# Where the sums of tokens, a product, copies of x and the counts of C stand in a Fourier-mixing and MLP kernel

## The chip, the cores and the metric

The kernel runs on 1 core of one Trainium2 chip. The metric is the device time of one execution in microseconds (us); the table below has the median of three runs. The program is compiled ahead; every engine (TensorE or PE, VectorE or DVE, ScalarE or ACT, GpSimd or POOL, SyncE or SP) works through its own queue of instructions in a fixed order and waits on semaphores.

## The reference

All in float32, with x of 2048 tokens by 576. `A_*` are the matrices of a discrete Fourier transform over the hidden and over the sequence dimension, `B_w1` is 576 by 4608, `B_w2` 4608 by 576.

```python
xn = _layernorm(x)                                   # no scale, no bias
a = einsum("bsd,ed->bse", xn, dft_hid_re)
b = einsum("bsd,ed->bse", xn, dft_hid_im)
y = einsum("ts,bse->bte", dft_seq_re, a) - einsum("ts,bse->bte", dft_seq_im, b)
h = maximum(einsum("bsd,df->bsf", xn, w1), 0)
return x + y + einsum("bsf,fd->bsd", h, w2)
```

## The kernel before, in words

Every float32 operand is split into two float16 parts, hi and lo, and each product is three float16 matmuls (hi by hi, hi by lo, lo by hi), summed in PSUM.

The tokens are 16 tiles of 128, in 4 groups of 4 tiles (`G` = 512 tokens). The hidden width of the MLP is cut into 9 blocks of 512. The outer loop, `steps`, runs over blocks b = 0 to 8 and inside over groups g = 0 to 3. At step (b, g) the program issues the first products `mlp1` of (b, g), interleaved with the second products `mlp2` of the step before it.

- `mlp2(b, g, n)`, n = 0 to 6, are the seven products of a Strassen-Winograd scheme. Products 0, 2, 3 and 6 are evacuated from PSUM by ScalarE (line 603), 1, 4 and 5 are added by VectorE (line 606). Products that share a PSUM place must wait until the one before them on that place has been read: 2 waits for the evacuation of 0, 4 for that of 2, and 6 for VectorE's addition of 4. GpSimd then adds the results to a buffer in DRAM, `spill` (line 609), which starts as a copy of x (`copy_x`, line 802, on SyncE's queue).
- `mlp1_out` (lines 388 to 404) turns the PSUM of `mlp1` into h and its four sums: ScalarE writes hi, VectorE lo.
- In blocks 0 and 1 `mlp1` is plain. From block 2 (`BB`) on it too is a Strassen-Winograd product (`pair_products`, line 515), and for that it needs sums of quarters of the transposed tokens. `sums_x(g)` makes them for group g: four sums, each 2 or 3 VectorE operations (lines 472 to 476), one ScalarE operation for hi (line 455) and one VectorE operation for lo (line 460). They go to `acc`, whose old content has been spilled by then. For groups 0 to 2 the temporary lies in a part of `dbuf`, and all of it is issued in block 1, one piece for each piece of work that takes a token from `owed_t`. For group 3 the temporary is `tsum`, the single buffer (tag `first`) that the counts use, and its pieces are issued in block 2 (`t_sum`).
- The counts: before the sequence transform the program needs a scale for each of 16 units of the matrices C. `first_c(m)` loads a block of C into the single buffer, `sum_c(m)` sums its absolute values on ScalarE (line 1012). `passes` is the list of such pairs. It starts in block 1, pauses while group 3's sums use the buffer (`PAUSE`), and goes on with two passes a group from step (2, 2).
- `prepare_block(b + 1)` is a list of small pieces that load, scale and split the weights of the next block: `load_w1`, `max_w1` (line 115), an all-reduce on GpSimd (line 121), `split_w1` (line 184), `load_w2`, `sum_w2` (line 683) and so on. `work()` issues the next piece.
- Step (0, 2), n = 2 in the loop, also normalizes tiles 12 to 15 (`normalize`, lines 258 and 259; `remainder`, lines 265 and 268) and transposes them by DMA (line 282).

The order in each queue is made by a scheduler from the order in which the program issues work. `tc.issue_after(x)` and `behind(key)` only keep what is inside from standing ahead of x, or of the last instruction recorded under that key; they add no wait of their own.

Of the kernel before, what the change touches and what calls it, by code (L numbers as in the profile page):

```python
# [49 lines left out]
def kernel(  # L50
# [47 lines left out]
    def load_raw(key, src, shape):  # L98
        r = raws[key] = raw.tile(shape, F32, tag="raw", name="raw_" + "_".join(map(str, key)))
        nc.sync.dma_start(r, src)  # L100
# [337 lines left out]
    def sums_x(g):  # L438

        if g < NG - 1:

            f = [w[:, 2 * KT * P :][:, : 2 * GH] for w in w1bufs[2:]]
        else:
            w = mlp.tile([P, HK, P], F32, tag="first", name="tsum", bufs=1)
            w = w.rearrange("p a b -> p (a b)")
            f = [w[:, k : k + 2 * GH] for k in (0, 2 * GH)]
        f = [w.rearrange("p (k t) -> p k t", t=GH) for w in f]  # L450
        tt = nc.vector.tensor_tensor

        def high(q):
            with tc.issue_after(gates[g][0]):
                nc.scalar.activation(xsums[g][:, q, 0], f[q % 2], AF.Copy)

        def low(q):
            hi, lo = (xsums[g][:, q, n] for n in range(2))
            with tc.issue_after(gates[g][1] if g < NG - 1 else order["vfree"]):
                tt(lo, f[q % 2], hi, ALU.subtract)  # L460

        for q, (head, tail) in enumerate((
            ((0, 1), (0, 0)), ((1, 1), None), ((1, 0), None), ((1, 1), (0, 1)),
        )):
            if q > 1:
                low(q - 2)
            t = f[q % 2]
            h, l = halves(g, head)
            with behind("vfree" if g == NG - 1 else None):
                if tail:  # L470
                    h2, l2 = halves(g, tail)
                    tt(t, h, h2, ALU.subtract)
                    tt(t, t, l2, ALU.subtract)
                else:
                    tt(t, h, f[1 - q % 2], ALU.subtract)
                tt(t, t, l, ALU.add)
# [136 lines left out]
    def max_w1(b, f):  # L613

        i, r = divmod(f, 2)
        if f == 0:
            mx["w1", b], sc["w1", b], pw["w1", b] = cell("mw1"), cell("sw1"), cell("pw1")
        if r == 0:
            mx["f", b] = cell("mf", 2)
        with behind("vfree" if b >= BB else "vfree" if f > 1 and b else ("sh", 12) if b  # L620
                    else ("sh", 1) if f > 1 else None):
            magnitude(mx["f", b][:, r : r + 1], raws["w1", b, i][:, r * KT : (r + 1) * KT])
        if r:
            if b:
# [3 lines left out]
            nc.vector.tensor_reduce(m, mx["f", b], AX.X, ALU.max)  # L628
# [282 lines left out]
    copy_x(2)  # L911
    mlp2(0, 0, 0)
# [13 lines left out]

    owed_t = [1] * 10 * (NG - 1)
# [73 lines left out]
    def first_c(m):  # L1001
        n, q = divmod(m, 4)
        f = firsts[m] = mlp.tile([P, HK, P], F32, tag="first", name=f"f{n}_{q}", bufs=1)
        with tc.issue_after(order["td"]):
            nc.sync.dma_start(f, blocks_c(n)[q])

    def sum_c(m):
# [19 lines left out]
    for n in range(2, len(steps)):  # L1027
# [26 lines left out]
        if b >= BB:  # L1054
# [10 lines left out]
            for do, q in (  # L1065
                (first, P1), (first, P2), (m, 0), (end, 0), (first, P6),
                (brief, 1), (first, P5), (end, 0), (later1, P2), (m, 1), (t_sum, 0),
                (ready, 1), (second, P1), (first, P7), (ready, 1), (m, 2), (second, P2),
                (t_sum, 0), (count, 0), (brief, 1), (first, P3), (first, P4), (later1, P7), (m, 3),
                (second, P6), (later1, P3), (later1, P4), (later2, P2), (brief, 1), (m, 4),  # L1070
                (t_sum, 0), (second, P5), (ready, 1), (m, 5), (end, 0), (second, P7),
                (t_sum, 0), (end, 0), (brief, 1), (m, 6), (count, 0), (brief, 2),
# [5 lines left out]
        for i in range(NF):  # L1078
            if n == 2:
                ps.append(early.pop(0) if early else mlp1(b, g, i))  # L1080
# [17 lines left out]
            if n == 2:  # L1098
                if i == 2:
                    todo += prepare_block(1)  # L1100
                for _ in range(6):
                    work()
                continue
            if b:
                work()
            for q in range(2 * i, min(2 * i + 2, 7)):
                mlp2(pb, pg, q)
                if b:
                    if owed_t:
                        owed_t.pop()  # L1110
                        next(tq, None)
# [3 lines left out]
            if b and i == 3 and owed_t:  # L1115
                owed_t.pop()
# [249 lines left out]
```

## Time and profile before

| what | value |
|---|---|
| median of 3 runs (1254.05 to 1255.16) | 1254.05 us |
| the profiled execution's own time | 1253.33 us |
| its span | 1251.6 us |
| TensorE busy | 1229.5 us (98%) |
| VectorE busy | 1008.3 us (81%) |
| ScalarE busy | 704.4 us (56%) |
| GpSimd busy | 158.1 us (13%) |
| granted TensorE clock, mean | 1.0 |

Times in the profile count from the start of the span. A row of the timeline has a start, a length, the engine, the line of the program, the operation, output and inputs, sizes, a count, and in brackets how long the engine had been idle before it and which instruction ended that. "x28" merges 28 instructions that follow one another. A row's length reaches past the start of the next one, since instructions overlap a little.

### The profile page before, as it was taken

The page shows a single profiled execution, that of the slowest core. Times are in us where ns is not written, and L with a number is a line of the kernel's source. Part 1 is how long each engine was busy: PE and PEld are TensorE (multiplying, and loading weights), DVE is VectorE, ACT ScalarE, POOL GpSimd, SP SyncE. Part 2 cuts the span into 40 slices and gives each one's busy share as a digit, 9 for nine tenths or more (in the row PEclk, how much of TensorE's full clock was granted, in tenths as well). Part 3 has the DMA queues.
Part 4 walks back from the last instruction along what each step waited for, and adds up shares of the span by engine and source line. Part 5 has one row for each costly group of instructions (what it writes and reads, how often), then busy time and mean ns, then how long its engine had stood idle before and what let it go on. Part 6 is the DMA issues. An engine that isn't in the chain of part 4 may idle for free.

```text
span 1251.6 us, 25268 instructions
## 1 busy us (share of the span) xinstructions
PE 1229.5 (98%) x10269; PEld 980.5 (78%) x10269; DVE 1008.3 (81%) x1919; ACT 704.4 (56%) x1192; POOL 158.1 (13%) x207
## 2 busy tenths in 40 slices
PE   8999999899999999999999999999999999999998
PEld 7655557788888888888888888877777777777776
DVE  8998986988878788788787878557787878888885
ACT  5655565566667666766766766546543333333332
POOL 2421121212121111111121212200000000000000
PEclk9999999999999999999999999999999999999999
DMA  8895475456667665766576666630053434443420
GB/s 311 166 183 113 94 136 122 78 110 143 132 120 170 126 150 116 137 140 137 117 160 136 140 147 117 114 89 1 1 173 120 136 109 155 128 132 123 137 87 20
DMA packets 80324, 157.28 MB, mean 126 GB/s; under 512 B 22224, under 2 KB 41168, under 8 KB 80208
## 3 DMA queue, kind: packets, MB, share of 16 engines
q1 hardware_dynamic: 57424, 113.20, 28.2%
q0 software_dynamic: 22784, 42.48, 25.1%
q8 instruction: 80, 1.31, 0.4%
q14 instruction: 36, 0.29, 0.1%
HBM read 104.53 MB, written 51.90 MB: 125 GB/s over the span
## 4 chain that ended last, share of the span: by engine, by line
PE 81%; DVE 13%; DMA 2%; ACT 2%; issue 2%; SPq 0%; POOL 0%; DVEq 0%; ACTq 0%; POOLq 0%
PE p L1298 26%; PE p L592 23%; PE bank L515 22%; PE pd L1169 8%; DMA raw_w<-in_w_dram 1%; PE p L344 1%; DVE w2s L184 1%; DVE c_mf L115 1%; DVE h L393 1%; DVE st L207 1%; DVE w1buf L184 1%; DVE h L404 1%; DVE h L537 0%; DMA f<-in_cre_dram 0%; DVE dbuf L258 0%
## 5 line engine op out<-in xcount | busy, mean ns | idle before, releaser
L592 PE MATMUL p<-w2s,h 128*128 128x288 f16 x3024 | 409.3, 286 | 9.8 <-ACT acc L603 2.3
L592 PEld LDWEIGHTS <-h 128*128 128x128 f16 x3024 | 295.4, 98 | 87.4 <-issue 12.7
L1298 PE MATMUL p<-R,cs 128*128 128x288 f16 x2688 | 329.4, 286 | 0.0
L1298 PEld LDWEIGHTS <-cs 128*128 128x128 f16 x2688 | 263.0, 98 | 66.3
L183 ACT ACTIVATE cs<-c,sc_c 128x1024 f16<-128x1024 f32 x112 | 125.2, 1144 | 196.7 <-DVE c L1231 72.6
L184 DVE SCALAR_TENSOR_TENSOR cs<-c,sc_c,cs 128x1024 f16<-128x1024 f32 x112 | 141.0, 1282 | 54.4 <-ACT cs L183 54.4
L515 PEld LDWEIGHTS <-w1buf 128*128 128x128 f16 x1600 | 156.5, 98 | 23.9 <-issue 2.8
L515 PEld LDWEIGHTS <-dbuf 128*128 128x128 f16 x1200 | 117.4, 98 | 15.8
L515 PE MATMUL bank<-xT,w1buf 128*128 128x256 f16 x832 | 109.8, 273 | 0.0
L515 PE MATMUL bank<-acc,w1buf 128*128 128x256 f16 x768 | 102.3, 273 | 2.1 <-DVE acc L545 1.1
L1169 PE MATMUL pd<-dbuf,xT 128*128 128x288 f16 x832 | 103.8, 286 | 0.0
L537 DVE TENSOR_TENSOR h<-s,h 128x1024 f16<-128x1024 f32 x56 | 68.6, 1224 | 37.9 <-ACT h L534 37.9
L1169 PEld LDWEIGHTS <-xT 128*128 128x128 f16 x832 | 80.8, 98 | 22.0 <-issue 1.9
L609 POOL DMA_DIRECT2D spill<-dbuf x70 | 61.1, 879 | 244.7 <-DVE dbuf L606 218.8
L522 ACT ACTIVATE h<-acc 128x256 f16<-128x256 f32 x112 | 46.0, 411 | 65.9 <-DVE acc L545 64.4
L515 PE MATMUL bank<-xT,dbuf 128*128 128x256 f16 x624 | 82.3, 273 | 0.0
L534 ACT ACTIVATE h<-s 128x1024 f16<-128x1024 f32 x56 | 59.2, 1056 | 36.8 <-DVE s L529 36.5
L515 PE MATMUL bank<-acc,dbuf 128*128 128x256 f16 x576 | 76.6, 273 | 0.0
L1304 DVE SCALAR_TENSOR_TENSOR o<-p,us_c,o 128x288 f32<-128x288 f32 x112 | 57.6, 514 | 12.9 <-PE p L1298 12.5
L1012 ACT ACTIVATE f<-f 128x1024 f32<-128x1024 f32 x60 | 62.8, 1046 | 2.5 <-DMA f<-in_cre_dram 2.5
L603 ACT ACTIVATE dbuf<-p,c_ub 128x576 f32<-128x576 f32 x70 | 51.2, 734 | 22.4 <-PE p L592 21.2
L609 POOL DMA_DIRECT2D spill<-sum x42 | 36.8, 877 | 183.5 <-DVE sum L606 164.9
(169 smaller groups left out, 1531.8 us busy)
## 6 DMA issues: line engine op xcount, KB each, us to landing
spill<-dbuf POOLq DMA_DIRECT2D x70, 288.0 KB, 5.2
c<-in_cre_dram SPq DMA_DIRECT2D x32, 512.0 KB, 4.3
c<-in_cim_dram SPq DMA_DIRECT2D x32, 512.0 KB, 4.8
f<-in_cre_dram SPq DMA_DIRECT2D x30, 512.0 KB, 5.4
f<-in_cim_dram SPq DMA_DIRECT2D x30, 512.0 KB, 5.6
spill<-sum POOLq DMA_DIRECT2D x42, 288.0 KB, 4.5
raw_w<-in_w_dram SPq DMA_DIRECT2D x17, 640.0 KB, 5.8
raw_w<-in_w_dram SPq DMA_DIRECT2D x18, 576.0 KB, 4.4
```

Of the source, the lines that this page charges most:

```text
L183: nc.scalar.activation(hi, src, AF.Copy, scale=s).ins,
L184: nc.vector.scalar_tensor_tensor(lo, src, s, hi, ALU.mult, ALU.subtract).ins,
L515: nc.tensor.matmul(ps, l, r, start=first and m == 0, stop=m == len(todo) - 1, skip_group_check=not first,)
L534: order["s"] = nc.scalar.activation(hi_s, st[:, 1:], AF.Copy).ins
L537: order["lo"] = nc.vector.tensor_tensor(lo_s, st[:, 1:], hi_s, ALU.subtract).ins
L592: order["pe"] = nc.tensor.matmul(ps[:, c], h[:, x, qa, c * P : (c + 1) * P], w[:, y, qb], start=first and i == 0 and j == 0, stop=i == NQ ...
L603: freed(nc.scalar.activation(o, ps, AF.Copy, scale=us[b]))
L609: nc.gpsimd.dma_start(spill[g, row, col], o, accum_op=ALU.add)
L1012: nc.scalar.activation(f, f, AF.Abs, scale=2.0**-10, accum_out=sums_c[:, n, q : q + 1])
L1169: nc.tensor.matmul(ps[j], xT[g][:, kx, c * P : (c + 1) * P], dsp[j][:, hl, k], start=(t % 2 == 0 and n == 0), stop=(t % 2 == 1 and n == le ...
L1298: nc.tensor.matmul(ps, w[:, a, k], r[:, c, rq], start=first and k == 0 and j == 0, stop=k == HK - 1 and j == 2, skip_group_check=not first,)
L1304: order["o"] = nc.vector.scalar_tensor_tensor(o, ps, us["c"][:, n : n + 1], o, ALU.mult, ALU.add).ins
```

## The change: five edits to the order of work

1. At step (0, 2) products 0 and 1 of `mlp2(0, 1)` are issued ahead of the last `mlp1(0, 2, 3)`. Tile 15's normalization stands behind the evacuation of that product 0 (`after="free"`), and the pieces of `work()` are 1 at i = 2 and 11 at i = 3 in place of 6 at each. The first `max_w1` of block 1 stands behind tile 15's remainder (`("E", 15)`) in place of the statistics (`("sh", 12)`).
2. `copy_x(3)` is issued next to `copy_x(2)`, ahead of the loads of w1 of block 1.
3. The sums of all four groups use the temporary in `dbuf`, and are all issued in block 1: one after each of the seven `mlp2` of a step, and 1 and 2 more at i = 1 and i = 3, so ten a step. `t_sum` and `owed_t` are gone.
4. The first count's load stands behind the loads of w2 of block 1 (`order["loads"]`) in place of the last transpose.
5. The counts have no pause. They begin at step (1, 2), i = 3, run two a group from step (2, 0) on, and one more pass stands in the tail behind product 3.

```diff
@@ load_raw
-        nc.sync.dma_start(r, src)
+        ins = nc.sync.dma_start(r, src).ins
+        if key[:2] == ("w2", 1):
+            order["loads"] = ins
@@ sums_x
-        if g < NG - 1:
-
-            f = [w[:, 2 * KT * P :][:, : 2 * GH] for w in w1bufs[2:]]
-        else:
-            w = mlp.tile([P, HK, P], F32, tag="first", name="tsum", bufs=1)
-            w = w.rearrange("p a b -> p (a b)")
-            f = [w[:, k : k + 2 * GH] for k in (0, 2 * GH)]
-        f = [w.rearrange("p (k t) -> p k t", t=GH) for w in f]
+        f = [
+            w[:, 2 * KT * P :][:, : 2 * GH].rearrange("p (k t) -> p k t", t=GH) for w in w1bufs[2:]
+        ]
...
-            with tc.issue_after(gates[g][1] if g < NG - 1 else order["vfree"]):
+            with tc.issue_after(gates[g][1]):
                 tt(lo, f[q % 2], hi, ALU.subtract)
...
-            with behind("vfree" if g == NG - 1 else None):
@@ max_w1
-        with behind("vfree" if b >= BB else "vfree" if f > 1 and b else ("sh", 12) if b
+        with behind("vfree" if b >= BB else "vfree" if f > 1 and b else ("E", 15) if b
                     else ("sh", 1) if f > 1 else None):
@@ ahead of the loop
     copy_x(2)
+    copy_x(3)
     mlp2(0, 0, 0)
...
-    owed_t = [1] * 10 * (NG - 1)
@@ first_c
-        with tc.issue_after(order["td"]):
+        with behind("loads"):
             nc.sync.dma_start(f, blocks_c(n)[q])
@@ passes
-    PAUSE = 4 + 2 * NG
     passes = [
-        lambda m=m: (sum_c(m - 1) if m not in (4, PAUSE) else None, first_c(m))
-        for m in range(4, 4 * len(units))
+        lambda m=m: (sum_c(m - 1) if m > 4 else None, first_c(m)) for m in range(4, 4 * len(units))
     ]
-    passes.insert(2 * NG, lambda: sum_c(PAUSE - 1))
@@ the loop, blocks from BB on
-            t_sum = lambda q: b == BB and g < NG - 1 and next(tq, None)
-            count = lambda q: (b, g) >= (BB, NG - 2) and passes and passes.pop(0)()
-            if (b, g) == (BB, 0):
-                passes.pop(0)()
+            count = lambda q: passes and passes.pop(0)()
...
@@ the loop, blocks 0 and 1
             if n == 2:
+                if i == 3:
+                    mlp2(pb, pg, 0)
+                    mlp2(pb, pg, 1)
                 ps.append(early.pop(0) if early else mlp1(b, g, i))
...
-                normalize(t)
+                normalize(t, after="free" if i == 3 else None)
...
-            if n == 2 and i == 3:
-                mlp2(pb, pg, 0)
-                mlp2(pb, pg, 1)
...
-                if i == 2:
-                    todo += prepare_block(1)
-                for _ in range(6):
-                    work()
+                if i > 1:
+                    todo += prepare_block(1) if i == 2 else []
+                    for _ in range(1 if i == 2 else 11):
+                        work()
...
-                    if owed_t:
-                        owed_t.pop()
-                        next(tq, None)
+                    next(tq, None)
...
-            if b and i == 3 and owed_t:
-                owed_t.pop()
+            for _ in range((0, 1, 0, 2)[i] if b else 0):
                 next(tq, None)
...
-            if n > 3 and i % 2 and passes:
+            if (n, i) > (6, 1) and i % 2 and passes:
                 passes.pop(0)()
         if n == 2:
-            copy_x(3)
             for q in range(2, 7):
...
@@ the tail
         if ends:
             ends.pop(0)()
+        if q == 3 and passes:
+            passes.pop(0)()
```

More of the change, by code (lines that the diff above doesn't have):

```diff
@@ L468, in sums_x @@
             h, l = halves(g, head)
-            with behind("vfree" if g == NG - 1 else None):
[L470 to L476, printed above, removed]
+            if tail:
+                h2, l2 = halves(g, tail)
+                tt(t, h, h2, ALU.subtract)
+                tt(t, t, l2, ALU.subtract)
+            else:
+                tt(t, h, f[1 - q % 2], ALU.subtract)
+            tt(t, t, l, ALU.add)
             yield
@@ L1060 @@
             brief = lambda q: [work(True) for _ in range(q)]
[L1061 to L1064 removed]
+            count = lambda q: passes and passes.pop(0)()
             for do, q in (
                 (first, P1), (first, P2), (m, 0), (end, 0), (first, P6),
[L1067 removed]
+                (brief, 1), (first, P5), (end, 0), (later1, P2), (m, 1),
                 (ready, 1), (second, P1), (first, P7), (ready, 1), (m, 2), (second, P2),
[L1069 removed]
+                (count, 0), (brief, 1), (first, P3), (first, P4), (later1, P7), (m, 3),
                 (second, P6), (later1, P3), (later1, P4), (later2, P2), (brief, 1), (m, 4),
[L1071 to L1072 removed]
+                (second, P5), (ready, 1), (m, 5), (end, 0), (second, P7),
+                (end, 0), (brief, 1), (m, 6), (count, 0), (brief, 2),
                 (second, P3), (second, P4), (later2, P7), (later2, P3), (later2, P4), (brief, 1),
```

## The prediction

> **What bounds the kernel now.** I read the page's busy shares first, then a table of busy time by stage, then TensorE's rows in order of time for every gap, and last VectorE's and ScalarE's rows around each gap.
>
> ```profile
> PE 1229.5 (98%) x10269; PEld 980.5 (78%) x10269; DVE 1008.3 (81%) x1919; ACT 704.4 (56%) x1192; POOL 158.1 (13%) x207
> ```
>
> TensorE (PE) is busy for 98% of the span, and the change gives it exactly the same matmuls; only 14 of them move. What can change is the time in which it waits. The table by stage (columns: stretch, its length, then busy us of PE, weight loads, DVE, ACT and POOL, the granted clock, the DMA share, GB/s) shows where that is:
>
> ```profile
> 84.00:106.00 22.00, 21.40 (x134) 12.48 (x133) 18.85 (x43) 12.11 (x21) 4.24 (x6) 1.00 0.70 183
> 106.00:154.00 48.00, 45.95 (x282) 26.59 (x281) 46.61 (x87) 26.12 (x44) 9.04 (x9) 1.00 0.58 112
> 154.00:177.00 23.00, 22.23 (x140) 13.34 (x140) 18.71 (x39) 14.97 (x26) 4.18 (x6) 1.00 0.61 123
> 177.00:205.00 28.00, 27.99 (x190) 18.03 (x188) 22.22 (x45) 17.26 (x28) 6.25 (x8) 1.00 0.67 127
> 205.00:250.00 45.00, 41.32 (x352) 34.39 (x352) 36.88 (x81) 24.94 (x52) 7.66 (x10) 1.00 0.49 92
> 250.00:805.00 555.00, 554.33 (x4805) 469.59 (x4804) 448.40 (x988) 376.30 (x734) 97.60 (x125) 1.00 0.65 135
> ```
>
> PE idles 0.60, 2.05, 0.77 and 0.01 us in the four stretches up to 205, 3.68 us from 205 to 250, and 0.67 us in the 555 us behind them. VectorE (DVE) has only 3.15, 1.39 and 4.29 us free in the first three, 8.83 us in all: block 1 is nearly bound by VectorE. The granted clock is 1.00 in every stretch, so no part of the argument hangs on it. The gaps that the edits touch, in PE's order of time (columns: start, length, engine, line, operation, count, and in brackets the idle time before it with its releaser):
>
> ```profile
> 64.94 6.21 PE L344 MATMUL p<-xT,w1buf 128*128 128x512 f16 x28
> 70.98 3.10 PE L592 MATMUL p<-w2s,h 128*128 128x288 f16 x24
> 75.63 1.63 PE L592 MATMUL p<-w2s,h 128*128 128x288 f16 x12 [1.54 <-ACT acc L603]
> ...
> 154.01 1.63 PE L592 MATMUL p<-w2s,h 128*128 128x288 f16 x12 [1.07 <-DVE dbuf L606]
> ...
> 172.81 1.63 PE L592 MATMUL p<-w2s,h 128*128 128x288 f16 x12 [0.76 <-ACT sum L603]
> ...
> 220.93 1.63 PE L592 MATMUL p<-w2s,h 128*128 128x288 f16 x12 [1.62 <-DVE sum L606]
> ...
> 223.98 0.81 PE L515 MATMUL bank<-acc,w1buf 128*128 128x256 f16 x6 [0.54 <-DVE half L124]
> ...
> 246.89 0.81 PE L515 MATMUL bank<-acc,w1buf 128*128 128x256 f16 x6 [1.14 <-DVE acc L545]
> ```
>
> **Edit 1: group 1's first products ahead of the third group's last.** The 28 matmuls at 64.94 are `mlp1(0,2,2)` and `mlp1(0,2,3)`; the 24 behind them are products 0 and 1 of `mlp2(0,1)`. The second half of the 28, some 3.0 us, moves behind the 24. Products 0 and 1 then end at about 71.0 instead of 74.0, their evacuations have 3.0 us more before product 2, and the 1.54 us at 75.63 goes; in ScalarE's queue the first evacuation now stands ahead of the normalizations. What is late next is product 6, which adds to the bank that VectorE's L606 of product 4 must first read. VectorE's rows there:
>
> ```profile
> 82.18 0.82 DVE L606 SCALAR_TENSOR_TENSOR acc<-p,c_ub,acc 128x576 f32<-128x576 f32 x1
> 82.91 1.23 DVE L404 TENSOR_TENSOR h<-s,h 128x1024 f16<-128x1024 f32 x1
> ```
>
> In the built order of the changed kernel the 1024-wide L404 that starts at 82.91 stands ahead of this L606, and two tiny scale operations stand behind it. Back to back the next operation starts some 0.1 us before such a row ends, so L404 takes 1.13 us of the queue, less about 0.14 for the two: L606 starts 1.0 us later, at 83.2, if VectorE has no gap before it in either kernel (its rows just ahead show none). Product 6, for which PE without its earlier waits is ready near 80, starts when that L606 ends: at about 84.1 instead of 83.1 (82.18 + 0.82, and a little). **So this edit, alone, moves a wait to VectorE and costs 1.0 us at that point.** The gates of `max_w1` (behind E of tile 15) and of `normalize(15)` (behind the evacuation) only set this order; tile 15's transposes come no later by my count, so they add nothing. If VectorE's own waits on ScalarE's normalizations show up, the cost grows to at most the 1.54 us that went.
>
> **Edit 2: the copies of x ahead of w1's loads.** On SyncE's queue the four `copy_x(3)` and the first count load stand ahead of w2's loads; the changed queue has the copies at the end of the transposes of group 2, ahead of w1's loads, and the count load behind w2's. The rows of SyncE's queue, of ScalarE's second sum over w2, and of what VectorE then waits for:
>
> ```profile
> 79.93 3.76 SPq L802 DMA_DIRECT2D spill<-in_x_dram  x4
> 83.74 0.60 SPq L1005 DMA_DIRECT2D f<-in_cre_dram  x1
> 85.75 5.62 SPq L100 DMA_DIRECT2D raw_w<-in_w_dram  x2
> ...
> 97.44 1.16 ACT L683 ACTIVATE j<-raw_w 128x1152 f32<-128x1152 f32 x1 [2.04 <-DMA raw_w<-in_w_dram]
> ...
> 99.22 0.69 DVE L393 SCALAR_TENSOR_TENSOR h<-p,h 128x512 f16<-128x512 f32 x1 [1.88 <-ACT h L392]
> ...
> 120.29 0.82 DVE L115 TENSOR_REDUCE c_mf<-raw_w 128x1 f32<-128x640 f32 x1 [0.97 <-DMA raw_w<-in_w_dram]
> ```
>
> The second w2 load is issued near 91 (85.75 + 5.62) and lands just before 97.44, some 6.2 us, with copies and a count load queued ahead of it. The page's row of such loads has a median of 4.4 us to landing:
>
> ```profile
> raw_w<-in_w_dram SPq DMA_DIRECT2D x18, 576.0 KB, 4.4
> ```
>
> At between 4.4 and 5.5 us it lands 1 to 2 us earlier, and ScalarE's queue behind it is free sooner. The 1.88 us gap then closes, because VectorE, 1.0 us behind and with more sums ahead, gets there at about 98.2, after ScalarE. Of the 3.15 us of VectorE's idle time from 84 to 106 I leave 0.4. The 1.39 us from 106 to 154 stays (0.97 of it waits for w1's load, which is tied to a buffer that VectorE frees). The copies themselves now run ahead of w1's loads, which wait there for buffers that VectorE has yet to free; nothing else waits for them. Cost there 0; what it would be if they held w1's loads up is bounded by their own 3.76 us of issue, and VectorE's first use of w1 lies far behind.
>
> **Edit 3: all sums of tokens in block 1.** The fourth group's sums are 14 more VectorE operations 512 wide and 4 on ScalarE, moved from block 2 into block 1; the counts that ran in block 1 leave ScalarE.
>
> ```profile
> L476 DVE TENSOR_TENSOR dbuf<-dbuf,xT 128x512 f32<-128x512 f32 x12 | 8.2, 687 | 0.1
> ...
> 130.33 1.29 DVE L460 TENSOR_TENSOR acc<-dbuf,acc 128x512 f16<-128x512 f32 x2
> ```
>
> One takes 0.69 us, and in a pair the second adds 0.60, so I count 0.60 in a dense queue: 8.4 us. What matters is how much more stands ahead of each L606 on which PE waits. By the built order it is: 2.7 us more ahead of the L606 behind the gap at 154.01 (four sums and a 256-wide operation), and 7.5 us more ahead of the one that releases the next product 6, which starts near 177 (172.81, 12 matmuls and 13 more; thirteen sums, less one such operation). Against that stands idle time that goes: by 154, 3.15 falling to 0.4 (edit 2), so 2.75 us; the two cancel, and the gap at 154.01 stays as it is. By 177, 2.75 plus the 4.29 of 154 to 177, which are waits on ScalarE that VectorE, being later, no longer meets (three of ScalarE's counts are gone from there): 7.0 us against 7.5, so 0.5 us late; the 0.76 us at 172.81, an evacuation that in the changed order stands ahead of ScalarE's L402, goes. I take **0 for everything up to 177**, with bounds of -2.0 (every gap up to there but one closes) and +7.5 (no idle time goes). From 177 to 205 VectorE has 5.8 us free, which covers the last 0.9 us of sums.
>
> **Block 2 without the sums.** Here the sums shared the count's single buffer.
>
> ```profile
> 210.86 1.06 ACT L1012 ACTIVATE f<-f 128x1024 f32<-128x1024 f32 x1 [2.46 <-DMA f<-in_cre_dram]
> ...
> 212.04 0.69 DVE L472 TENSOR_TENSOR tsum<-xT 128x512 f32<-128x512 f16 x1 [2.95 <-ACT f L1012]
> ```
>
> VectorE stood 2.95 us behind a count, which stood 2.46 us behind its load; VectorE is late from there on, and PE waits on it at 220.93, 223.98 and 246.89: 1.62 + 0.54 + 1.14 = 3.3 us. With the buffer left to the counts, VectorE waits for none of them, and it has 8.4 us less to do. The pattern becomes that of 250 to 805 (two counts a group), where PE idles 0.67 us in 555. I take **-3.3**, between 0 and -3.6.
>
> **Counts later.** One more pass runs at the very end: the last count's load now follows the count before it, some 9 us later than now, and the count ends near 816.
>
> ```profile
> 818.55 0.50 ACT L1189 ACTIVATE c<-pd,c_rho 128x288 f32<-128x288 f32 x1 [4.95 <-DMA spill<-sums]
> ```
>
> ScalarE's next work waits until 818.55 for the last spill anyway, so the cost is 0; if that cover is gone it is at most the 1 us or so by which the count's load slows that spill, and PE needs those banks only with the next pair of tiles.
>
> **The sum.** Profiled execution 1253.33 us (span 1251.6 and 1.7 around it), 0.7 below the median of the runs, 1254.05. 0 - 3.3 + 0 = -3.3, laid on the median: **1250.7 us**.
>
> **Rivals.**
>
> *VectorE bounds block 1, and the end is later.* The waits of VectorE from 84 to 177 do not shrink, because they hang on ScalarE and on loads. Each microsecond of the 8.8 that stays beyond 1.3 (8.8 less 7.5) goes onto PE by 177. If all stay: +7.5 - 3.3 = +4.2, 1258.3 us. It is slower by over 2.5 us once some 7 of the 8.8 remain. For it: VectorE's 97% from 106 to 154. Against: the largest wait follows the w2 load, which the edit frees, and ScalarE sheds its counts. Chance 0.16.
>
> *Block 2 keeps its waits.* Counts now run there two to a group, and a count that waits for its load holds ScalarE's evacuations. Then 0 in place of -3.3: 1254.0 us. Against: the stretch from 250. With half of it, or half the first rival, the time stays within 2.5 us of before; chance 0.22.
>
> *More goes than I count.* Product 6 waits no longer than now, and the gaps at 154 and 172 close: -2.0 - 3.3 and the 1.0 of edit 1: 1247.8 us. Chance 0.10.
>
> *GpSimd is held up by the added sums.*
>
> ```profile
> L121 POOL PARTITION_ALL_REDUCE top<-c_mw x24 | 9.8, 408 | 83.6 <-DVE c_mw L628 44.8 <-ACT j L683 38.9
> ```
>
> VectorE waits for such a reduction of 0.41 us before it scales each weight; five of these fall among the sums. Should each be held for one 0.69 us sum, VectorE is 3.4 us later by 177 and the gain is gone: 1254.1 us. [...] Chance 0.04.
>
> *The change doesn't do what it says.* The order is set by a scheduler; but the built order has all sums of tokens ahead of block 2's first product. Chance 0.01.
>
> **How the numbers follow.** The forecast, 1248.5 to 1251.5, has 0.47. Faster by over 0.2% (2.5 us, about what a measurement of this kernel can tell from no change) are the forecast and the third rival: 0.57. Within 0.2%: the second, the fourth and the fifth, 0.27. Slower: 0.16. The range reaches from 1247.5, below the third rival, to 1257.0, where the first rival is cut near its end; some 0.15 is left out. The forecast's own range is 1248.5 to 1251.5.
>
> **What would show it.** Right: no gap at 75; product 6 of `mlp2(0,1)` waiting on L606 for 4 us or so; VectorE without a gap near 98; PE at the first product of block 2 within 1 us of before; from there to 250 no gap over 0.5 us. Wrong: VectorE idle over 3 us between 84 and 154, gaps on L606 in block 1 that sum to over 3 us more than now, or a wait on a count in block 2.

## The result, and the profile after

The changed kernel takes **1250.07 us** (median, 1249.30 to 1251.33) where the kernel before, run beside it, took 1253.53 us. The ratio is **0.9972, 95% interval 0.9961 to 0.9982**: faster by 0.28%, as forecast (1250.7). The profiled execution took 1249.30 us, with a span of 1247.5 us.

The table by stage of the changed kernel, with the columns of the one shown of before (length, then busy us of PE, weight loads, DVE, ACT, POOL, granted clock, DMA share, GB/s):

```profile
84.00:106.00 22.00, 22.00 (x133) 13.15 (x132) 21.00 (x45) 15.15 (x25) 5.40 (x6) 0.93 0.64 132
106.00:154.00 48.00, 45.66 (x286) 27.17 (x285) 46.41 (x88) 22.83 (x38) 9.21 (x9) 1.00 0.52 90
154.00:177.00 23.00, 22.76 (x143) 13.44 (x141) 22.72 (x45) 15.07 (x26) 4.46 (x6) 1.00 0.48 78
177.00:205.00 28.00, 27.75 (x188) 18.03 (x188) 23.09 (x48) 15.99 (x25) 6.08 (x7) 1.00 0.62 108
205.00:250.00 45.00, 44.71 (x389) 37.80 (x387) 35.48 (x79) 28.37 (x61) 7.58 (x10) 1.00 0.69 143
250.00:805.00 555.00, 554.33 (x4802) 469.35 (x4800) 443.34 (x977) 376.88 (x735) 97.94 (x125) 1.00 0.66 135
```

TensorE idles 0.29 us from 205 to 250 where it idled 3.68. VectorE's idle time in the first three stretches is 1.00, 1.59 and 0.28 us, 2.87 in all where it was 8.83: the added sums have filled it. The granted clock is 0.93 from 84 to 106, which it was in no stretch before.

TensorE's rows in order of time (start, length, line, count, idle time before and its releaser):

```profile
56.61 1.14 PE L589 MATMUL p<-w2s,h 128*128 128x288 f16 x8 [0.93 <-DVE w2s L186]
...
70.34 3.18 PE L346 MATMUL p<-xT,w1buf 128*128 128x512 f16 x14
73.36 6.04 PE L589 MATMUL p<-w2s,h 128*128 128x288 f16 x48
83.50 3.04 PE L589 MATMUL p<-w2s,h 128*128 128x288 f16 x12 [4.10 <-DVE c_sw L127]
...
89.43 3.10 PE L589 MATMUL p<-w2s,h 128*128 128x288 f16 x24
...
130.61 1.63 PE L589 MATMUL p<-w2s,h 128*128 128x288 f16 x12 [0.98 <-DVE acc L603]
...
150.01 1.63 PE L589 MATMUL p<-w2s,h 128*128 128x288 f16 x12 [1.36 <-ACT dbuf L600]
...
177.25 1.63 PE L589 MATMUL p<-w2s,h 128*128 128x288 f16 x12 [0.47 <-DVE sum L603]
...
200.87 1.69 PE L512 MATMUL bank<-xT,w1buf 128*128 128x256 f16 x14
...
205.44 0.81 PE L512 MATMUL bank<-acc,w1buf 128*128 128x256 f16 x6 [0.29 <-ACT acc L538]
...
218.66 0.82 PE L512 MATMUL bank<-acc,w1buf 128*128 128x256 f16 x6
219.31 1.63 PE L589 MATMUL p<-w2s,h 128*128 128x288 f16 x12
...
799.87 0.53 PE L1156 MATMUL pd<-dbuf,xT 128*128 128x288 f16 x3
```

(L589, L600, L603, L512 are L592, L603, L606, L515 of the kernel before.) The gap at 75 is gone: products 2 to 5 run as one row of 48. Product 6 waits 4.10 us, and then its 12 matmuls take 3.04 us where they took 1.63. The bracket names the tiny L127; the addition of product 4, whose place product 6 needs, ended just then too, at 82.64 + 0.81 = 83.45:

```profile
82.64 0.81 DVE L603 SCALAR_TENSOR_TENSOR acc<-p,c_ub,acc 128x576 f32<-128x576 f32 x1
83.37 0.14 DVE L127 TENSOR_SCALAR c_sw<-half 128x1 int32<-128x1 int32 x1
```

Block 2 has no wait but 0.29.

These two executions do not start alike (the first row above is at 56.61 us, its twin of before at 57.18), so all traces below are compared by three lengths: from the row with the wait of 0.93 for `w2s` to the first product of block 2 (56.61 and 200.87 above); from there to the first matmul of the transform (799.87); from there to the end of the span. The three rows of before:

```profile
57.18 1.14 PE L592 MATMUL p<-w2s,h 128*128 128x288 f16 x8 [0.93 <-DVE w2s L184]
...
200.71 1.69 PE L515 MATMUL bank<-xT,w1buf 128*128 128x256 f16 x14
...
803.89 0.53 PE L1169 MATMUL pd<-dbuf,xT 128*128 128x288 f16 x3
```

Before: 143.53, 603.18, 447.71 us. Against these, in us, with the ratio of the timed runs:

| kernel | up to block 2 | block 2 to the transform | rest | ratio to before, 95% |
|---|---|---|---|---|
| changed | +0.73 | -4.18 | -0.08 | 0.9972 (0.9961 to 0.9982) |
| b_sums | +1.16 | -2.90 | -0.15 | 0.9974 (0.9963 to 0.9984) |
| a_order_back | +1.07 | -4.14 | -0.07 | 0.9972 (0.9961 to 0.9982) |
| a_copies_back | +1.95 | -4.18 | -0.13 | 0.9973 (0.9963 to 0.9983) |
| b_order | +0.54 | +1.15 | -0.02 | 1.0003 (0.9994 to 1.0012) |
| b_pause | -0.02 | -2.61 | +1.14 | 0.9998 (0.9989 to 1.0007) |
| b_pause_tail | +0.02 | -2.61 | +0.26 | 0.9980 (0.9971 to 0.9989) |
| a_vec_first | +1.30 | -3.83 | -0.07 | 0.9971 (0.9960 to 0.9982) |
| a_p6_late | -3.03 | -2.97 | -0.05 | 0.9955 (0.9942 to 0.9967) |
| a_p6_fill | +1.07 | -4.20 | -0.05 | 0.9969 (0.9958 to 0.9979) |
| a_fill | +2.12 | -3.95 | -0.08 | 0.9982 (0.9973 to 0.9991) |
| a_wait5 | -0.40 | -4.54 | -0.20 | 0.9956 (0.9944 to 0.9969) |
| p6_wait5 | -1.63 | -3.28 | -0.12 | 0.9951 (0.9938 to 0.9963) |

Each length comes from one execution, and the executions of one kernel lie 0.7 to 3.5 us apart (`b_sums` was profiled in the slowest of its eight, 1251.18 us, `b_pause` in the fastest of its eleven, 1251.44), so a microsecond in it says little by itself; the ratios decide. An `a_` kernel is the changed one with an edit, a `b_` kernel the one before.

### The profile page after: what moved, and what is told of

It is laid out like the page before. It is cut to its first block, busy times and chain, and to the rows that moved or that the text cites. A ratio compares the mean times of both kernels' runs of the same rounds, so it can differ in the third digit from the quotient of the medians.

```text
span 1247.5 us, 25273 instructions
## 1 busy us (share of the span) xinstructions
PE 1228.4 (98%) x10269; PEld 981.0 (79%) x10269; DVE 1009.1 (81%) x1919; ACT 704.7 (56%) x1192; POOL 158.9 (13%) x207
## 4 chain that ended last, share of the span: by engine, by line
PE 83%; DVE 7%; ACT 1%; issue 1%; DMA 1%; POOL 0%; POOLq 0%; DVEq 0%; ACTq 0%
PE p L1285 26%; PE p L589 24%; PE bank L512 23%; PE pd L1156 8%; DMA raw_w<-in_w_dram 1%; PE p L346 1%; DVE w2s L186 1%; DVE h L395 1%; DVE dbuf L473 1%; DVE acc L458 0%; DVE c_mf L117 0%; PE pd L1166 0%; DVE w1buf L186 0%; ACT f L1008 0%; DVE dbuf L470 0%
## 5 line engine op out<-in xcount | busy, mean ns | idle before, releaser
L589 PE MATMUL p<-w2s,h 128*128 128x288 f16 x3024 | 410.2, 287 | 9.2 <-DVE c_sw L127 4.1
L589 PEld LDWEIGHTS <-h 128*128 128x128 f16 x3024 | 296.1, 98 | 86.0 <-issue 10.6
L512 PEld LDWEIGHTS <-w1buf 128*128 128x128 f16 x1600 | 156.5, 98 | 21.6 <-issue 0.5
L512 PEld LDWEIGHTS <-dbuf 128*128 128x128 f16 x1200 | 117.4, 98 | 15.8
L512 PE MATMUL bank<-xT,w1buf 128*128 128x256 f16 x832 | 109.8, 273 | 0.0
L512 PE MATMUL bank<-acc,w1buf 128*128 128x256 f16 x768 | 102.3, 273 | 0.3 <-ACT acc L538 0.3
L606 POOL DMA_DIRECT2D spill<-dbuf x70 | 61.0, 874 | 241.7 <-DVE dbuf L603 214.6
L512 PE MATMUL bank<-xT,dbuf 128*128 128x256 f16 x624 | 82.3, 273 | 0.0
L512 PE MATMUL bank<-acc,dbuf 128*128 128x256 f16 x576 | 76.6, 273 | 0.0
L600 ACT ACTIVATE dbuf<-p,c_ub 128x576 f32<-128x576 f32 x70 | 51.3, 733 | 22.3 <-PE p L589 22.0
L520 DVE SCALAR_TENSOR_TENSOR h<-acc,h 128x256 f16<-128x256 f32 x112 | 47.3, 422 | 18.7 <-ACT h L519 18.3
```

Source lines behind the costliest of these rows:

```text
L512: nc.tensor.matmul(ps, l, r, start=first and m == 0, stop=m == len(todo) - 1, skip_group_check=not first,)
L589: order["pe"] = nc.tensor.matmul(ps[:, c], h[:, x, qa, c * P : (c + 1) * P], w[:, y, qb], start=first and i == 0 and j == 0, stop=i == NQ ...
L600: freed(nc.scalar.activation(o, ps, AF.Copy, scale=us[b]))
L606: nc.gpsimd.dma_start(spill[g, row, col], o, accum_op=ALU.add)
```

## The experiments

**Which edits carry the gain.** Theory: the sums and the counts carry it; what edit 1 loses on TensorE is taken up later by VectorE. Rival: each edit counts at its own place on TensorE's path, edit 1 as a loss, edit 2 as a gain.

`b_sums` leaves edits 1 and 2 (and the place of the first count's load) as before and takes the rest of the change:

```diff
 # before, with sums_x, tq, passes and count of the change; unchanged are:
     copy_x(2)                 # copy_x(3) stays at the end of step (0, 2)
     ps.append(...mlp1(0, 2, 3)); mlp2(0, 1, 0); mlp2(0, 1, 1)
     with tc.issue_after(order["td"]): ...   # first count's load
```

> The kernel before with the sums and the counts of the change alone (edit 3, block 2, counts later), without edit 1 and without edit 2. By the prediction's terms block 2 gives -3.3, edit 1's +1.0 (+1.4 of clock) is not there, and without edit 2 the 1.9 us wait of VectorE near 98 us stays, so 7.5 us of sums stand against 5.1 of idle time: +1.9 to +2.4. Sum -0.9 to -1.4: 1252.2 us, ratio 0.999. Rival: edit 2 is worth nothing on TensorE's path, and edit 1 costs what it shows: then -3.3 to -4, 1250 us or less, ratio 0.997 or below. In both no wait of TensorE over 0.5 us between 206 and 250 us.

Measured: 1249.62 us, ratio 0.9974, the changed kernel's own. In its trace block 2 keeps waits of 0.48 and 0.44 us. The prediction's terms (1252.2) were off, and the rival of that text came in: by the times, sums and counts alone give the whole gain.

`a_order_back` undoes edit 1 in the changed kernel:

```diff
-                if i == 3:
-                    mlp2(pb, pg, 0)
-                    mlp2(pb, pg, 1)
                 ps.append(early.pop(0) if early else mlp1(b, g, i))
-                normalize(t, after="free" if i == 3 else None)
+                normalize(t)
                 transposes_dma(t, nc.scalar)
+            if n == 2 and i == 3:
+                mlp2(pb, pg, 0)
+                mlp2(pb, pg, 1)
```

> The changed kernel with edit 1 undone (products 0 and 1 of group 1 again behind mlp1(0,2,3), with the gates and the pieces of work that go with that order). TensorE's path: in the changed kernel product 6 waits 4.1 us and its 12 matmuls then take 3.04 us instead of 1.63, so edit 1 costs 1.0 + 1.4 us; without it the kernel takes 2.4 us less than the changed one, near 1247.7 us, ratio to before 0.995. Rival, VectorE's path: VectorE is full from 100 to 177 us and every later wait of TensorE is one for VectorE, so what edit 1 loses at 89 us is taken up by shorter waits at 130 and 150 us; then within 0.7 us of the changed kernel, ratio 0.997, and the waits behind 100 us are longer. In both the granted clock is 1.00 from 84 to 106 us.

Measured: 1249.68 us, 0.9972. Product 6 starts after a wait of 0.78 us and takes 1.63, and yet nothing is won: a wait of 1.23 us follows (the bracket names no instruction; the same row of `b_sums` waits 1.33 us for the transposes' DMA), and the one at 150 is 1.71 us instead of 1.36, as the second reading has it. TensorE's rows of this kernel:

```profile
82.50 1.63 PE L589 MATMUL p<-w2s,h 128*128 128x288 f16 x12 [0.78 <-DVE acc L603]
...
85.36 2.97 PE L346 MATMUL p<-xT,w1buf 128*128 128x512 f16 x13 [1.23 <-issue]
...
150.29 1.63 PE L589 MATMUL p<-w2s,h 128*128 128x288 f16 x12 [1.71 <-ACT dbuf L600]
```

`b_order` does edit 1 alone in the kernel before (the diff above the other way round).

> The kernel before with edit 1 alone (the product order, with its gates and pieces of work). By the prediction's term +1.0 us, with the drop of the clock that the changed kernel shows +2.4: 1253.9 to 1255.3 us where before takes 1252.9, ratio 1.0008 to 1.002. By the other reading, in which VectorE's chain of w2's scale and w1's load of block 2 is reached near 117 us in every kernel whatever TensorE did ahead of it, TensorE's loss at 83 to 89 us is gone by 130 us: ratio 1.000, with product 6 late by 1.0 us or more and the later waits shorter.

Measured: 1254.01 us, 1.0003. Its product 6 waits 4.10 us and takes 3.04, exactly as in the changed kernel; its clock is 0.95 from 60 to 84 us and 0.90 from 84 to 106, some 2.4 + 4.4 = 6.8 us at half, against 3.41 there (83.50 to 86.91). Up to block 2 its trace shows +0.54 us. A loss of 2.4 us (1.0019) is excluded by the interval; one of 1.0 is not, by this run alone.

`a_copies_back` undoes edit 2 and the place of the first count's load:

```diff
     copy_x(2)
-    copy_x(3)
...
-        with behind("loads"):
+        with tc.issue_after(order["td"]):
...
         if n == 2:
+            copy_x(3)
```

> The changed kernel with edit 2 undone (the copies of x and the first count's load again ahead of w2's loads). By the prediction the second w2 load lands 1 to 2 us later, and VectorE waits 1.9 us near 98 us instead of 0.9; counted as the prediction counts it, this is 1 to 2 us of the sums' cover, 1251 to 1252 us, ratio 0.998 to 0.9985. If VectorE is brought to the same place at 120 us by w1's load anyway, no difference: 0.997.

Measured: 1250.11 us, 0.9973: no difference, the second reading. VectorE's wait near 98 is 0.94 us there and 0.93 in the changed kernel; edit 2 does not touch it. Edit 1 does: with it alone (`b_order`) the wait is 1.18 us, and in the changed kernel without it (`a_order_back`) 2.23.

**What made block 2 wait.** `b_pause` is the kernel before, with the fourth group's sums still in block 2 but no count ahead of them in their buffer:

```diff
-    PAUSE = 4 + 2 * NG
+    PAUSE = 4 + 2 * NG - 1
...
-    passes.insert(2 * NG, lambda: sum_c(PAUSE - 1))
+    passes.insert(2 * NG - 1, lambda: sum_c(PAUSE - 1))
...
-            if (b, g) == (BB, 0):
-                passes.pop(0)()
```

> The kernel before with one count fewer in block 1: the last count before the fourth group's sums runs at the end of block 1, so these sums, still in block 2, wait for no count and no load; one more count runs at the end. If it was the shared buffer that made VectorE late in block 2 (2.95 us behind a count), the waits of TensorE at 220.9, 224.0 and 246.9 us go, and the kernel is 3.3 us faster than before: 1250.2 us, ratio 0.9974. If it was the 8.4 us of sums themselves, the three waits stay and the time is that of before, ratio 1.000; a part of each gives a time between.

Measured: 1252.76 us, 0.9998. By the time alone that looks like the second answer; the trace, of its fastest execution, says otherwise. The waits at 220.9 and 224.0 are gone, the third stays (1.15 us at 243.76), block 2 is 2.61 us shorter, and behind 805 us, where one count more now runs, 1.14 are lost again:

```profile
243.76 0.81 PE L515 MATMUL bank<-acc,w1buf 128*128 128x256 f16 x6 [1.15 <-DVE acc L545]
...
821.69 0.28 PE L1167 MATMUL pd<-dbuf,xT 128*128 128x288 f16 x1 [0.22 <-DVE R L1196]
822.35 6.16 PE L1167 MATMUL pd<-dbuf,xT 128*128 128x288 f16 x49 [0.38 <-DVE R L1196]
```

So the same kernel was run with one of the counts at the end moved behind product 3, as the change has it (`b_pause_tail`):

```diff
     for q in range(7):
         mlp2(*steps[-1], q)
...
+        if q == 3 and passes:
+            passes.pop(0)()
```

> The kernel before with its last count before the fourth group's sums at the end of block 1, as in the earlier run, and one of the counts at the very end issued behind product 3 of the last group, as the changed kernel has it. The earlier run's trace showed 2.6 us less in block 2 and 1.15 us more behind 805 us. If the extra count at the very end was the 1.15 us, it goes here: 1250.4 us, ratio 0.998, and TensorE has no wait between 805 and 920 us. If the gain in block 2 was of that one execution alone, the ratio is 1.000 again.

Measured: 1250.77 us, 0.9980, and no wait between 805 and 920. So the buffer that the sums shared with the counts cost about 2.5 us (1 - 0.9980, and 2.61 in the trace) of the 3.5 that the whole change gives. What is left in block 2, 4.18 - 2.61 = 1.57 us in the traces, is for the most part the third wait, for an addition of VectorE, which here still has the 8.4 us of sums in block 2. And one count too many at the very end costs some 2 us by the medians (1252.76 against 1250.77; 1.14 - 0.26 = 0.88 by the two traces), which the pass behind product 3 saves.

**The wait of product 6, and the clock.** `a_vec_first` moves the four reductions of w1 and the 1024-wide L406 behind product 4's addition on VectorE:

```diff
-                    for _ in range(1 if i == 2 else 11):
+                    for _ in range(1 if i == 2 else 0):
                         work()
...
             for q in range(2, 7):
                 mlp2(pb, pg, q)
+                if q == 4:
+                    for _ in range(11):
+                        work()
+                    late_lo()        # L406 of mlp1_out(0, 2, 1)
...
-        with behind(... ("E", 15) if b ...):
+        with behind(... "vfree" if b ...):
```

> The changed kernel with what stood ahead of product 4's addition on VectorE moved behind it: the four reductions of w1 (3.0 us) and the 1024-wide L406 (1.1 us). Product 6 then waits for VectorE for 0.5 to 1 us instead of 4.1, no drop of the clock follows, and mlp1(0,3,0) waits for its transposes until 82 us. TensorE is 3 to 4 us ahead at 84 us. If TensorE's waits there are what block 1 costs: 1246.5 us, ratio to before 0.995, as for the kernel with product 6 behind mlp1(0,3,0). If VectorE's chain (w1's scales come 3 us later here) sets block 1: no gain, 1249.7 us, or slower, with new waits of TensorE at mlp1(1,0,0) and behind it.

Measured: 1249.46 us, 0.9971: no gain. Product 6 starts at 80.31 after 0.55 us, and the time comes back as a wait of 3.44 us at 115.62:

```profile
80.31 1.63 PE L595 MATMUL p<-w2s,h 128*128 128x288 f16 x12 [0.55 <-DVE acc L609]
...
115.62 1.86 PE L595 MATMUL p<-w2s,h 128*128 128x288 f16 x7 [3.44 <-DVE h L395]
```

`a_fill` puts 64 matmuls of zeros into the 4.1 us (nothing of the output uses them):

```diff
             for q in range(2, 7):
+                if q == 6:
+                    held.append(new_ps1(0, 3, 0))
+                    with behind("pe"):
+                        for _ in range(64):
+                            nc.tensor.matmul(held[0][:, :P], idle, idle, start=True, stop=True)
                 mlp2(pb, pg, q)
```

> The changed kernel with 64 matmuls of zeros (128 wide, some 3.6 us) in the 4.1 us in which TensorE waits ahead of product 6; they write a bank that mlp1(0,3,0) then clears, and the result does not use them. The granted clock stays 1.00 and the 12 matmuls take 1.63 us instead of 3.04. If the drop of the clock is lost time, the gain is 1.4 us: 1248.3 us, ratio 0.996. If VectorE takes it up, 0.997 as the changed kernel, the later waits being longer.

Measured: 1251.54 us, 0.9982. The clock is 1.00 from 60 to 106 us and the 12 matmuls take 1.63 us; the time is not shorter. With the 64 matmuls in TensorE's queue the scheduler also orders VectorE's queue otherwise behind them (product 5 of the next group then waits 2.23 us at 104.56), so the run keeps the clock and changes the order at once: it does not show what the clock alone is worth.

`a_p6_late` issues product 6 behind `mlp1(0,3,0)`:

```diff
         if n == 2:
-            for q in range(2, 7):
+            for q in range(2, 6):
                 mlp2(pb, pg, q)
...
                     mlp1_step(b, g, i, ps)
+                if n == 3 and i == 0:
+                    mlp2(0, 1, 6)
```

> The changed kernel with product 6 of mlp2(0,1) issued behind mlp1(0,3,0), which then fills part of the 4.1 us wait. mlp1(0,3,0) needs the four transposes, which land near 82 us, so TensorE idles some 2.9 us ahead of it and not at all ahead of product 6. TensorE's path: no drop of the clock, and TensorE reaches mlp2(0,2,0) near 87.0 instead of 89.4; 2.4 us faster than the changed kernel, ratio to before 0.995. VectorE's path: TensorE is early there and waits longer at the later products, within 0.7 us of the changed kernel, ratio 0.997. If the clock drops after 2.9 us of idling too, a granted clock under 1.00 shows between 82 and 86 us.

Measured: 1246.95 us (1245.86 to 1249.31), 0.9955. It is faster than the changed kernel, but not for the reason on record: the clock did drop, after 2.40 us (0.63 from 82 to 84 us and 0.52 from 84 to 86), and `mlp1(0,3,0)` takes 4.65 us, so TensorE comes to `mlp2(0,2,0)`, the thirteenth matmul of the row of 36, near 88.6, 31.8 us behind the common mark (56.83) and only 1.0 ahead of the changed kernel (89.43 - 56.61 = 32.8), where 2.4 was expected. The rest comes further on: from 90 to 200 us it has no wait over 0.20, and block 1 is 3.76 us shorter than the changed kernel's.

```profile
82.02 4.65 PE L346 MATMUL p<-xT,w1buf 128*128 128x512 f16 x13 [2.40 <-issue]
...
87.14 4.58 PE L589 MATMUL p<-w2s,h 128*128 128x288 f16 x36
```

`a_p6_fill` fills that wait with 36 matmuls of zeros:

```diff
         if i == 0:
             ps.append(new_ps1(b, g, 0))
+            if (b, g) == (0, 3):
+                for _ in range(36):
+                    nc.tensor.matmul(ps[0][:, :P], idle, idle, start=True, stop=True)
```

> The kernel with product 6 behind mlp1(0,3,0), with 36 matmuls of zeros (128 wide, some 2.0 us) in the 2.4 us in which TensorE waits for the transposes; they write the bank that mlp1(0,3,0) then clears, and the result does not use them. If it is idling that costs the clock, the granted clock is 1.00 from 78 to 90 us, mlp1(0,3,0) takes 2.97 us instead of 4.65, and the median falls by up to 1.7 us, to 1245.5 (0.994). If a wait on VectorE takes that up, it stays near 1246.9 (0.9955).

Measured: 1249.71 us, 0.9969. The clock is 1.00 from 60 to 106 us and the row of 13 takes 2.96 us, and the gain of `a_p6_late` is gone: again VectorE's queue stands in another order, and the waits at 120 (0.88 us, VectorE) and 150 (1.42 us, TensorE) are back.

**VectorE's wait at 120 us.** In ten of the fourteen traces (all but `a_vec_first`, `a_p6_late` and the two below) VectorE waits 0.6 to 1.6 us for one load near 120 us: block 2's first w1, whose buffer comes free when block 1's w2 has been split. The rows of VectorE in the changed kernel and, in the second box, in `a_order_back`:

```profile
117.21 0.81 DVE L603 SCALAR_TENSOR_TENSOR acc<-p,c_ub,acc 128x576 f32<-128x576 f32 x1
...
119.96 0.82 DVE L117 TENSOR_REDUCE c_mf<-raw_w 128x1 f32<-128x640 f32 x1 [1.27 <-DMA raw_w<-in_w_dram]
...
129.75 0.81 DVE L603 SCALAR_TENSOR_TENSOR acc<-p,c_ub,acc 128x576 f32<-128x576 f32 x1
```

```profile
120.00 0.82 DVE L117 TENSOR_REDUCE c_mf<-raw_w 128x1 f32<-128x640 f32 x1 [1.41 <-DMA raw_w<-in_w_dram]
...
129.31 0.81 DVE L603 SCALAR_TENSOR_TENSOR acc<-p,c_ub,acc 128x576 f32<-128x576 f32 x1
```

In all ten the addition comes 9.1 to 9.8 us behind this reduction. `a_wait5` moves the reduction behind the next additions:

```diff
 def prepare_block(b):
-        wait, wait2 = ([lambda: None] * n for n in ((2, 2) if b < BB else (3 + (b == BB), 0)))
+        wait, wait2 = ([lambda: None] * n for n in ((2, 2) if b < BB else (3 + 2 * (b == BB), 0)))
```

> The changed kernel with one more empty step ahead of block 2's first weight maximum, so that VectorE's reduction that waits 1.27 us for w1's load at 120 us stands behind the addition at 131 us, and sums stand in its place. If that wait, which every slow-anchored kernel shows at 120 us, is what brings them all to the same addition at 129.3 to 130.0 us, that addition starts some 1.4 us earlier, and the kernel gains 1.0 to 1.4 us on the changed one: ratio to before 0.996. If VectorE's whole work up to 177 us counts, the order within it does nothing: 0.997.

Measured: 1247.87 us (1247.68 to 1248.34), 0.9956. VectorE's rows have no wait there, and the addition comes 10.93 us behind the one at 118.39, where it took 12.54 in the changed kernel:

```profile
118.39 0.82 DVE L603 SCALAR_TENSOR_TENSOR acc<-p,c_ub,acc 128x576 f32<-128x576 f32 x1
...
129.32 0.81 DVE L603 SCALAR_TENSOR_TENSOR acc<-p,c_ub,acc 128x576 f32<-128x576 f32 x1
...
132.11 1.54 DVE L117 TENSOR_REDUCE c_mf<-raw_w 128x1 f32<-128x640 f32 x2
```

TensorE's waits of 0.98 and 1.36 us at 130.61 and 150.01 are gone, but for 0.21 at 147.34, though product 6 still waits 4.09 us at 84. The interval of the ratio overlaps the changed kernel's (0.9944 to 0.9969 and 0.9961 to 0.9982), but none of its times (up to 1248.34) reaches the changed kernel's lowest, 1249.30, nor that of `a_copies_back`, 1249.32, which ran beside it; the traces put the difference at 1.1 us up to block 2 and 0.4 in it. `p6_wait5` is `a_p6_late` with the same edit.

> The kernel with product 6 behind mlp1(0,3,0) (0.9955) with the same empty step. That kernel had no wait at 120 us, because its load landed by 118.5 us; so the step takes nothing away: 0.9955 again if the wait for the load is the whole matter, and if the order of the sums matters by itself, up to 1 us either way.

Measured: 1247.05 us, 0.9951 (0.9938 to 0.9963), the lowest ratio of all and below both kernels; against `a_p6_late` (0.9955) no difference that these runs can tell, as expected.

**Is that wait the place where edit 1's loss ends?** The theory in `b_order` and `a_copies_back` says so; the rows do not. These are two pairs of like rows of TensorE, first in the changed kernel, then in `a_order_back`:

```profile
93.00 2.98 PE L346 MATMUL p<-xT,w1buf 128*128 128x512 f16 x13
...
115.16 2.98 PE L346 MATMUL p<-xT,dbuf 128*128 128x512 f16 x13
```

```profile
91.73 2.98 PE L346 MATMUL p<-xT,w1buf 128*128 128x512 f16 x13
...
114.97 2.98 PE L346 MATMUL p<-xT,dbuf 128*128 128x512 f16 x13
```

By the common mark the changed kernel is 1.28 us late at the first and 0.20 at the second; `b_order` against the kernel before is 3.07 late at the first and 0.84 at the second. So most of the loss is gone by 115 us, ahead of VectorE's wait. The load that VectorE then waits for is issued 57.79 us behind the mark in the changed kernel and 57.68 in `a_order_back`: VectorE is level too by then (in `b_order` it is 0.83 late there). VectorE was free for 1.00 us from 84 to 106 in the changed kernel and for 3.04 in `a_order_back`; so the likeliest reading is that what edit 1 costs VectorE goes into idle time that VectorE has there anyway, above all near 98 us, though no run moved that idle time alone. `a_wait5` shows what the wait at 120 us costs, not that it levels the kernels.

## Why the prediction was right, and where it was not

- **The bound.** That TensorE's waits are the only thing to win, and that VectorE nearly bounds block 1, held.
- **Edit 1.** Its picture held to the hundredth: product 6 waits 4.10 us and starts 83.50 - 56.61 = 26.89 us behind the common mark, where before it was 83.06 - 57.18 = 25.88: the +1.0 us. Two things failed. The clock: "no part of the argument hangs on it" was read from a trace in which TensorE's longest idle time there is 1.62 us; with 4.10 it dropped to 0.50 from 83.50 to 86.91, and the next product (89.43) is late by 2.38 us. And the step from "late at that point" to the sum: the sum leaves this 1.0 us out and gives no reason. `b_order` and `a_order_back` bear the omission out, as they show no loss that can be told in the time: most of it is gone by 115 us, and VectorE idles less near 98.
- **Edit 2.** VectorE's gap near 98 shrank to 0.93 us and did not close; idle time from 84 to 106 is 1.00 us, not 0.4. But `a_copies_back` has the same gap of 0.94, so it wasn't the copies; `b_order` and `a_order_back` put it down to edit 1. The term was wrong in cause, and worth nothing in the time.
- **Edit 3, 0 up to 177.** The count of sums was right, 13 more started by 177 us (55 against 42), and TensorE gets to block 2 at 200.87 against 200.71 (+0.73 by the common mark). The four more by 153 us (40 against 36) were put down to this edit; `b_order` has 40 without it and `a_order_back` 36 with it, so they come from edit 1. And the 0 is a balance of other waits than those named: the 1.07 us at 154.01 did not stay but is gone, and 0.98 at 130.61 and 1.36 at 150.01 (for ScalarE) are new. The wait near 177 came in as worked out, 0.47 us for VectorE where 0.5 was forecast, and the 0.76 at 172.81 is gone.
- **Block 2, -3.3.** Right in mechanism, too small: -4.18. The idle times in brackets say less than a wait costs, since a row's length reaches some 0.16 us past the next row's start:

```profile
218.50 0.82 PE L515 MATMUL bank<-acc,w1buf 128*128 128x256 f16 x6
...
233.63 1.91 PE L515 MATMUL bank<-xT,w1buf 128*128 128x256 f16 x16
235.62 0.82 PE L515 MATMUL bank<-acc,w1buf 128*128 128x256 f16 x6
...
242.43 0.82 PE L515 MATMUL bank<-acc,w1buf 128*128 128x256 f16 x6
243.25 1.63 PE L592 MATMUL p<-w2s,h 128*128 128x288 f16 x12
```

  These are rows of the kernel before. From 218.50 to the product at 220.93 is 2.43 us, in the changed kernel 219.31 - 218.66 = 0.65: 1.78 us lost where the bracket says 1.62. Three such waits are 3.30 + 3 x 0.16, and two hitches with no bracket, 235.62 and 243.25, come to 0.25 and 0.17 us against the same rows elsewhere (1.74 and 0.65): 4.20 in all.
- **The tail, 0.** Right (-0.08), but not for want of a cost: `b_pause` shows the price of one count more at the end without the pass behind product 3.
- **The rivals.** VectorE did not bound block 1 (it fell short of the 7 us by far). GpSimd was held up little: five reductions from 84 to 206 us took 3.4 us in sum instead of 2.8 (columns: count, busy, mean ns):

```profile
L123 POOL PARTITION_ALL_REDUCE top<-c_mw x5 | 3.4, 671 | 12.1 <-ACT j L680 11.5 <-DVE c_mw L625 0.6
```

  Before, in the same stretch, the mean was 563 ns, so 0.5 us where the rival had 3.4. One reduction in the five is longer, by 0.47 us (1.28 where the longest of before took 0.81); that a sum holds such a reduction up no run here shows.

So the forecast came out at the right time with two of its terms wrong in size (block 2 by -0.9, block 1 by +0.7) and nearly cancelling, which is luck, and with a cost and a gain at edits 1 and 2 that do not reach the end.

## What to carry to other kernels

A delay of one engine is not a delay of the kernel: edit 1 made TensorE late by 2.4 us at 89 us, and most of that was gone by 115, as far as the rows tell because the engine that it then waits for, VectorE, had idle time to give. So follow a delay to the next place where another engine has idle time before laying it on the sum. A wait that most versions share, as VectorE's for w1's load (0.6 to 1.6 us in ten of the fourteen traces), is worth a try of its own: put the next work ahead of the waiting instruction. A buffer shared by two uses makes one of them wait for the other's load, and the price stands where the waiting engine is next needed, not where it waits (before, VectorE waited 2.95 us at 212.04, and TensorE's waits for it began at 220.93). And a count of idle times in brackets can fall short (3.30 us in block 2 of before, where 4.20 were lost); the starts of like rows in the two traces give the loss itself.

## What the hardware showed

TensorE's granted clock fell to half at some idle times and was back some 3.4 to 3.6 us later (the changed kernel, `a_p6_late`, `a_wait5`, `p6_wait5`) or 6.8 (`b_order`, `a_copies_back`, `a_vec_first`), as the means of the stretches give it. The stretches of the changed kernel around product 6, and of `a_vec_first` around its wait of 3.44 us (the clock is the figure behind POOL's count, third from the end):

```profile
82.00:84.00 2.00, 0.50 (x3) 0.32 (x3) 2.00 (x7) 0.46 (x1) 0.63 (x2) 0.87 0.33 74
84.00:86.00 2.00, 2.00 (x10) 1.30 (x9) 2.00 (x4) 1.09 (x2) 2.00 (x3) 0.50 0.30 20
86.00:88.00 2.00, 2.00 (x10) 0.94 (x9) 1.97 (x7) 1.42 (x2) 1.26 (x2) 0.77 1.40 152
```

```profile
114.00:116.00 2.00, 0.38 (x2) 0.28 (x3) 2.00 (x5) 2.00 (x4) 0.00 (x0) 0.52 0.64 103
116.00:118.00 2.00, 2.00 (x9) 1.06 (x7) 2.00 (x5) 1.19 (x3) 0.00 (x0) 0.50 0.00 0
118.00:120.00 2.00, 2.00 (x5) 0.38 (x4) 2.00 (x4) 0.37 (x1) 0.00 (x0) 0.50 0.95 317
120.00:122.00 2.00, 2.00 (x8) 0.80 (x7) 0.93 (x2) 0.00 (x0) 1.08 (x1) 0.77 0.93 274
```

Behind 50 us it dropped at idle times of 4.10 us (the changed kernel, `b_order` and `a_copies_back`), 4.09 (`a_wait5`), 3.44 (`a_vec_first`), 2.40 (`a_p6_late`) and 2.39 (`p6_wait5`), and not at 2.23 (`a_fill`) or 2.02 (`b_order`, in block 2). With matmuls of zeros in the gap it was 1.00 from 60 to 106 us (`a_fill`, `a_p6_fill`).

In two of these runs the drop came ahead of the end of the idle time. `a_vec_first`'s TensorE stops at 112.18 us; its clock is 1.00 from 112 to 114 and 0.52 from 114 to 116, so at half from some 114.1, 1.9 us in. `b_order`'s TensorE stops at 79.40 and starts again at 83.50; its mean of 0.95 from 60 to 84 comes to some 2.4 us at half ahead of 84. Nor was one idle time always one price: the same 4.10 us cost 3.41 us of half clock in the changed kernel (83.50 to 86.91) and some 6.8 in `b_order`. With a drop 1.9 us into one idle time and none in one of 2.23, the length alone does not decide it here; what does, no run shows.

Left open: why the load that VectorE waits for at 120 us in ten of the traces lands by 118.5 us in `a_p6_late`, where the 4 us from 112 to 116 hold a DMA share of 0.62 and 0.29 against 0.95 and 1.05 in the changed kernel. From 106 to 122 us GpSimd issued three transfers to `spill` there and four in the changed kernel; no run moved them alone.
